# Moving the next expert's gather and transposes ahead of a tail, in an attention and mixture-of-experts kernel on one core

## The chip, the core and the metric

The kernel runs on one core of one Trainium2 chip. The metric is device time in microseconds (us) for one execution. A core has five engines that run side by side, each through its own instructions in program order, and that wait for each other by semaphores: PE (TensorE, the matrix unit; the profile shows its weight loads apart, as PEld), DVE (VectorE), ACT (ScalarE), POOL (GpSimd) and SP (SyncE, which here only issues DMAs). "SPq" in the profile is SP's queue.

## What is computed

The reference is a linear attention followed by a mixture of experts, each token going to two of eight experts:

```python
kv = np.einsum('bhsd,bhse->bhde', k, v)
out = np.einsum('bhsd,bhde->bhse', q, kv)
x = out / sqrt(mean(out * out) + 1e-6) * g_norm        # -> x: (4608, 512)
noisy = x @ w_gate + log1p(exp(x @ w_noise)) * noise   # 8 logits a token
top2, top2_w = the two largest and their softmax
for e in range(8):
    for k in range(2):
        mask = top2[:, k] == e
        h = np.maximum(x[mask] @ w1[e], 0.0)            # 512 -> 1024
        out[mask] += top2_w[mask, k, None] * (h @ w2[e])  # 1024 -> 512
```

Batch 8, 8 heads, 576 positions, head size 64: 4608 tokens of 512 values. The routing depends on the data, so how many tokens an expert gets is known only when the kernel runs (1152 on average).

## The kernel before, in words

**Two phases.** In the first 200 us or so the attention is computed, the logits, the routing, and the normalized tokens are written to memory (xs); the first units of expert 0 run inside it. After that the experts run one after the other. Only this second part matters here.

**Units and stages.** An expert's tokens are held in ten slots of 128 tokens (tiles). They are worked in units (list `units`, L344 to L349): experts 1 to 7 have two full units of four tiles and a tail of two, which I call A, B and T; expert 0 has four full units of two tiles and a tail. A unit goes through `gather` (L358: one indirect DMA a tile, issued from POOL, fetches token rows from xs into xg; five buffers), `halves` (L368: ACT casts a tile to half precision, POOL subtracts to get the remainder, both go to xh; four buffers), `xpose` (L375: one DMA transpose a tile, issued from SP, puts xh into xT; there are two xT buffers, which successive units alternate), `l1` (L414: first layer, matmuls at L427, evacuated from PSUM by ACT at L432 and DVE at L433 into hT) and `l2` (L465: second layer, matmuls at L473, ACT scales the result by the gate into y at L494, and `scatter`, L401, adds it to the output by an indirect DMA with addition from POOL, L405). PSUM tiles for all of this rotate over six buffers (`ps_tile`, L354).

A tail holds what is left of an expert's tokens. Its matmuls stand in a switch over the number of tokens in steps of 32 (L451), from none to 256, so a tail is short.

**Order of the work.** The program is issued in one order by the loop at L818; each engine takes its own part of it. For unit u it issues the gather of unit u+1, l1(u) and then l2(u-1). Around the tail the stages on PE follow each other as: l1(A), l2 of the tail before, l1(B), l2(A), l1(T), l2(B), l1 of the next expert's A. `l1` and `l2` are generators. A full unit yields 16 times in each of them (8 times for a unit of two tiles), a tail TY times in `l1` and twice in `l2`. After each yield the loop calls `fill()` (L772), which issues one step of background work.

**Halves and transposes** of unit u+1 are issued inside l1(u), after step XH = 5 and the next (L844). In a tail's l1 there are too few steps for that, so they follow after its last step (L846).

**Background work** is a queue of generators (`bg`). For the next expert it holds `locate` (L756), which finds the expert's tokens: it compares routing numbers on DVE (L309 to L314), counts with small matmuls into M (L322) and makes the lists of indices idx, row and gate (`finish`, L329). Then comes `prepare` (L750), which runs `weights` (L218). For each of the two raw weight matrices it takes the largest value (DVE, L225), spreads a scale over partitions by a small matmul of a diagonal dg (PE, L236, read by DVE at L238) and splits the float32 weights into two half-precision parts, a high one by ACT (L259) and a low one by DVE (L261, L263). A generator may yield a number n, and then the next n - 1 calls of `fill` do nothing for it.

**Raw weights** have one buffer for each layer (rw, 2 MB), filled by four DMAs of 512 KB from SP: `load_w1` (L207, DMAs at L210) and `load_w2` (L212, L216). The buffer is free when the last chunk has been split, so a load waits on SP for DVE's last split (L263), and whatever stands behind it in SP's queue waits too. In `weights`, the load of the next expert's first layer is issued right after the split of this one's first layer (L285), that of the second right after the split of the second (L293).

Of the kernel before, what the change touches and what calls it, by code (L numbers as in the profile page):

```python
# [24 lines left out]
E, FF = 8, 1024  # L25
# [21 lines left out]
XH = 5  # L47
FE = 2
GB, HB = 5, 4
GRAIN, TY, HINT = 32, 4, 5  # L50
PZ = 4


# [1 line left out]
def attention_moe(ctx: ExitStack, tc: tile.TileContext, kvm, kvr, qt, gn, wgn, noise, w1, w2, out):  # L55
# [7 lines left out]
    raw = ctx.enter_context(tc.tile_pool(name="raw", bufs=1))  # L63
# [141 lines left out]
    WT, RW, late = {}, {}, {}  # L205

    def load_w1(e):  # L207
        r = RW[e, 0] = raw.tile([P, 4, 1024], F32, name="rw")
        for c in range(4):
            SP.dma_start(r[:, c], w1[e, c * P:(c + 1) * P, :])  # L210

    def load_w2(e):  # L212
        r = RW[e, 1] = late.get("raw", raw).tile([P, 4, 1024], F32, name="rw")
        v = w2[e].rearrange("(c f p) d -> c p f d", f=2, p=P)
        for c in range(4):
            SP.dma_start(r[:, c].rearrange("p (f d) -> p f d", f=2), v[c])  # L216

    def weights(e, pool, lo, slack=0):  # L218
        WT[e] = w = {}
        sc = lists.tile([P, 8], F32, name="sc")  # L220

        def scale(o, src, mul):
            mx = lists.tile([P, 4], F32, name="mx")
            for c in range(4):
                V.tensor_reduce(mx[:, c:c + 1], src[:, c], axis=AX.X, op=OP.max, apply_absolute_value=True)  # L225
                yield
            V.tensor_reduce(sc[:, o:o + 1], mx, axis=AX.X, op=OP.max)
            if mul is not None:
                V.tensor_scalar(sc[:, o:o + 1], sc[:, o:o + 1], mul, None, op0=OP.mult)
            al = lists.tile([P, 1], F32, name="al")  # L230
            dg = lists.tile([P, P], F32, name="dg", bufs=1)
            V.tensor_scalar(dg, ident, sc[:, o:o + 1], None, op0=OP.mult)
            yield
            yield
            ps = ps_tile([P, P])
            T.matmul(ps, onef, dg, start=True, stop=True)  # L236
            yield
            V.tensor_reduce(al, ps, axis=AX.X, op=OP.max)  # L238
            V.tensor_scalar(al, al, 1e-30, 1e30, op0=OP.max, op1=OP.min)
            bi = lists.tile([P, 2], I32, name="bi")  # L240
            V.tensor_scalar(bi[:, 0:1], al.bitcast(I32), 0x7F800000, None, op0=OP.bitwise_and)
            V.tensor_scalar(sc[:, o + 1:o + 2].bitcast(I32), bi[:, 0:1], -1.0, float(257 << 23), op0=OP.mult, op1=OP.add)  # L242
            V.tensor_scalar(sc[:, o + 2:o + 3].bitcast(I32), bi[:, 0:1], 1.0, float(-(3 << 23)), op0=OP.mult, op1=OP.add)
            if mul is not None:
                V.scalar_tensor_tensor(sc[:, o + 1:o + 2], sc[:, o + 1:o + 2], -1.0, g, op0=OP.mult, op1=OP.mult)  # L245
            yield

        def split(src, hi, lw, s):
            if lo is G:
                for c in range(5):  # L250
                    if c:
                        G.tensor_tensor(lw[:, c - 1], src[:, c - 1], hi[:, c - 1], OP.subtract)
                    if c < 4:
                        A.activation(src[:, c], src[:, c], AF.Copy, scale=s)
                        A.activation(hi[:, c], src[:, c], AF.Copy)
                    yield
                return
            for c in range(4):
                A.activation(hi[:, c], src[:, c], AF.Copy, scale=s)  # L259
                if c:  # L260
                    lo.scalar_tensor_tensor(lw[:, c - 1], src[:, c - 1], s, hi[:, c - 1], op0=OP.mult, op1=OP.subtract)  # L261
                yield
            lo.scalar_tensor_tensor(lw[:, 3], src[:, 3], s, hi[:, 3], op0=OP.mult, op1=OP.subtract)  # L263
            yield
            yield

        if (e, 0) not in RW:
            load_w1(e)
            yield WY
            for _ in range(slack):  # L270
                yield
        r1 = RW.pop((e, 0))
        yield from scale(0, r1, gabs)
        w["w1h"] = pool.tile([P, 4, FF], F16, name="w1h")
        w["w1l"] = pool.tile([P, 4, FF], F16, name="w1l")
        yield from split(r1, w["w1h"], w["w1l"], sc[:, 1:2])
        for _ in range(min(slack, 3)):
            yield
        if (e, 1) not in RW:
            load_w2(e)  # L280
            yield WY
            for _ in range(slack):
                yield
        elif e + 1 < E:
            load_w1(e + 1)  # L285
        r2 = RW.pop((e, 1))
        yield from scale(3, r2, None)
        V.tensor_scalar(sc[:, 6:7], sc[:, 2:3], sc[:, 5:6], -1.0 / XS, op0=OP.mult, op1=OP.mult)
        w["c"] = sc[:, 6:7]
        w["w2h"] = pool.tile([P, 4, FF], F16, name="w2h")  # L290
        w["w2l"] = pool.tile([P, 4, FF], F16, name="w2l")
        yield from split(r2, w["w2h"], w["w2l"], sc[:, 4:5])
        if "raw" in late and e + 1 < E:  # L293
            load_w2(e + 1)
        for k in ("w2h", "w2l"):
            w[k] = w[k].rearrange("p c (f d) -> p (c f) d", f=2)

# [27 lines left out]
    def scale_gates(e, c):  # L325
        if "c" in WT.get(e, ()):
            V.tensor_scalar(LG[e][:, c], LG[e][:, c], WT[e]["c"], None, op0=OP.mult)
# [16 lines left out]
    units = []  # L344
# [9 lines left out]
    def ps_tile(shape):  # L354
        rot[0] = (rot[0] + 1) % 6
        return (psa if "ps" not in late or rot[0] < 2 else late["ps"]).tile(shape, F32, name="pp")
# [35 lines left out]
    def clear():  # L392
        r = next(blank, None)
        if r is not None:
            zeroed.append(A.dma_start(ov[:, r], zrow).ins)
            return True
# [124 lines left out]
    ready, loaded = {0}, set()  # L521
# [223 lines left out]
    late["ps"] = ctx.enter_context(tc.tile_pool(name="psb", bufs=4, space=PSUM))  # L745
    psl = ctx.enter_context(tc.tile_pool(name="psl", bufs=1, space=PSUM))
    bg = deque()
    hold = [0]

    def prepare(e):  # L750
        yield from weights(e, wts_b if e % 2 else wts_a, V)
        if e in ready:
            scale_gates(e, slice(0, CAP))
        loaded.add(e)

    def locate(e):  # L756
        M = psl.tile([P, 5 * CAP], F32, name="M")
# [10 lines left out]
    def background(e):  # L768
        yield from locate(e)
        yield from prepare(e)  # L770

    def fill():  # L772
        hold[0] -= 1
        if bg and hold[0] <= 0:
            try:
                hold[0] = next(bg[0]) or 1
            except StopIteration:
                bg.popleft()

    bg.append(prepare(1))  # L780
    k = 0
    while side:
# [35 lines left out]
    for u in range(EARLY, len(units) + 1):  # L818
        if u < len(units):
            e, tiles, tail = units[u]  # L820
            if u + 1 < len(units):
                en = units[u + 1][0]
                while en not in ready:
                    fill()
                if (u + 1, units[u + 1][1][0]) not in XG:
                    gather(u + 1)
                if units[u + 1][2]:
                    RV[en] = [nc.values_load(arms[0:1, i, en:en + 1], engines=(ET.PE,), min_val=0, max_val=m)
                              for i, m in enumerate((2 * P // GRAIN, 2))]
            if u > EARLY:  # L830
                while clear():
                    pass
                scatter()
            while e not in loaded:
                fill()
            if tiles[0] == 0 and e + 1 < E:
                bg.append(locate(e + 1))
                bg.append(prepare(e + 1))
            todo = deque([halves, xpose] if u + 1 < len(units) and u + 1 not in XT else ())
            for i, _ in enumerate(l1(u)):  # L840
                if i == HINT and u and units[u - 1][2]:
                    tc.switch_hint({ET.PE: RV[units[u - 1][0]][1]}, 3, label=f"down{units[u - 1][0]}")
                fill()
                if todo and i >= XH:  # L844
                    todo.popleft()(u + 1)
            while todo:  # L846
                todo.popleft()(u + 1)
        if u > EARLY:
            for i, _ in enumerate(l2(u - 1)):
                if i == HINT and u + 1 < len(units) and units[u + 1][2]:  # L850
                    en = units[u + 1][0]
                    tc.switch_hint({ET.PE: RV[en][0]}, 256 // GRAIN + 1, label=f"up{en}")
                if i == HINT and u + 1 == len(units):
                    tc.switch_hint({ET.PE: RV[e][1]}, 3, label=f"down{e}")
                fill()


# [69 lines left out]
```

## Time and profile before

| | us |
|---|---|
| median of 3 runs | 1046.17 |
| lowest, highest | 1027.74, 1051.88 |
| the profiled execution | 1023.48 |
| its span, first to last instruction | 1021.6 |
| mean granted PE clock, as a share | 0.957 |

The profile's page lists busy time by engine. "Busy" for PE is modelled, so a busy PE isn't PE at its peak. Other views show who waited for whom (engine, line, what it waited for: total us, times, longest), the instructions of an engine in order of time (start, duration, engine, line, operation, output <- inputs, shape, count, and in brackets the idle time before and what ended it), and busy times cut by stretches of the span (length, then busy us and instructions of each engine, the granted PE clock as a share, the mean busy share of the DMA engines, which can exceed 1, and GB/s).

### The profile page before, as it was taken

To read this page: it belongs to the slowest core of one execution; us is meant where nothing else is said; L and a number is where in the kernel's file an instruction comes from. 1 tells how busy PE (TensorE), PEld (TensorE's weight loads), DVE (VectorE), ACT (ScalarE), POOL (GpSimd) and SP (SyncE) were. 2 spreads that over 40 slices of the span, in tenths; PEclk is the share of its full clock that TensorE was granted. 3 is DMA by queue.
4 is the path that set the end of the run, shared out by engine and by line. 5 is a ranking of instruction groups with operands and counts; after the bars stand their busy time and mean duration, and the time that the engine had idled before them with its cause. 6 is when DMAs were issued, how large, how long until landed. Compare 5 with 4: busy or idle time off the path is not lost. (4 is left out here: it accounts for less than half of the span.)

```text
span 1021.6 us, 15198 instructions
## 1 busy us (share of the span) xinstructions
PE 920.9 (90%) x5962; PEld 516.6 (51%) x5962; DVE 497.8 (49%) x1046; ACT 331.1 (32%) x573; POOL 379.6 (37%) x398
## 2 busy tenths in 40 slices
PE   9957797898999979997999889997999989999995
PEld 8846774574444534463445434463444344644452
DVE  2869988855456333840555345632375257411100
ACT  2736662243223321341224322332133223421211
POOL 0214543445522642145223632263224541552222
PEclk9979988999999979998999989998999999999998
DMA  9988966966834864259244953357327842473224
GB/s 347 335 299 289 273 250 228 293 140 169 205 64 114 151 124 60 68 129 205 43 62 119 183 113 64 109 153 115 52 55 198 172 87 34 92 128 57 36 41 56
DMA packets 140826, 145.88 MB, mean 143 GB/s; under 512 B 90784, under 2 KB 99104, under 8 KB 140704
## 3 DMA queue, kind: packets, MB, share of 16 engines
q1 hardware_dynamic: 108192, 82.25, 30.3%
q0 software_dynamic: 17920, 41.95, 21.3%
q10 hardware_dynamic: 14592, 19.93, 5.8%
q8 instruction: 91, 1.49, 0.6%
q14 instruction: 31, 0.25, 0.1%
HBM read 83.02 MB, written 40.11 MB: 121 GB/s over the span
## 5 line engine op out<-in xcount | busy, mean ns | idle before, releaser
L427 PE MATMUL pp<-xT,w1h 128*128 128x512 f16 (+5 forms) x1600 | 370.2, 329 | 36.1 <-DMA xT<-xh 28.7
L473 PE MATMUL pp<-w2h,hT 128*128 128x512 f16 x1200 | 364.8, 381 | 1.9 <-ACT hT L432 1.2
L433 DVE SCALAR_TENSOR_TENSOR hT<-pp,hT 128x512 f16<-128x512 f32 x160 | 107.4, 687 | 404.1 <-ACT hT L432 404.1
L473 PEld LDWEIGHTS <-hT 128*128 128x128 f16 x1800 | 176.0, 98 | 212.8 <-issue 5.4
L405 POOL DMA_INDIRECT out_rows<-y,row x80 | 130.1, 1626 | 371.5 <-ACT y L494 354.6
L427 PE MATMUL pp<-xT,w1l 128*128 128x512 f16 (+5 forms) x800 | 257.5, 328 | 0.0
L473 PE MATMUL pp<-w2l,hT 128*128 128x512 f16 x600 | 228.7, 381 | 0.0
L427 PEld LDWEIGHTS <-w1h 128*128 128x128 f16 x1600 | 150.6, 99 | 147.2 <-issue 49.4
L432 ACT ACTIVATE hT<-pp 128x512 f16<-128x512 f32 x160 | 92.7, 597 | 317.5 <-PE pp L427 315.0
L372 POOL TENSOR_TENSOR xh<-xg,xh 128x512 f16<-128x512 f32 x80 | 114.4, 1456 | 118.7 <-ACT xh L371 118.7
L494 ACT ACTIVATE y<-pp,gate 128x512 f32<-128x512 f32 x80 | 53.9, 686 | 252.5 <-PE pp L473 226.8
L427 PEld LDWEIGHTS <-w1l 128*128 128x128 f16 x800 | 79.5, 99 | 58.0 <-issue 5.8
L364 POOL DMA_INDIRECT xg<-xs,idx x80 | 79.9, 998 | 35.1 <-issue 23.0
L225 DVE TENSOR_REDUCE mx<-rw 128x1 f32<-128x1024 f32 x64 | 74.4, 1208 | 11.3 <-DMA rw<-w 11.3
L585 PE MATMUL big<-kvbd,qt 128*128 128x160 f32 (+1 forms) x320 | 58.9, 337 | 14.9 <-ACT kvbd L577 12.5
L612 POOL TENSOR_TENSOR x<-o,ss 128x512 f32<-128x512 f32 x36 | 38.6, 1073 | 64.6 <-DVE ss L606 57.4
L585 PEld LDWEIGHTS big<-kvbd,qt 128*128 128x128 f32 (+1 forms) x320 | 49.3, 201 | 17.3 <-ACT kvbd L577 13.4
L371 ACT ACTIVATE xh<-xg 128x512 f16<-128x512 f32 x80 | 46.0, 629 | 23.0 <-DMA xg<-xs,idx 19.1
L309 DVE TENSOR_TENSOR oa<-jb,lnb 128x1152 bf16<-128x1152 bf16 x32 | 52.6, 1642 | 0.0
L259 ACT ACTIVATE w2h<-rw,sc 128x1024 f16<-128x1024 f32 x32 | 35.8, 1146 | 6.0 <-DVE sc L242 6.0
L404 POOL MEMSET tick<- 1x1 f32 x80 | 37.2, 465 | 0.0
L259 ACT ACTIVATE w1h<-rw,sc 128x1024 f16<-128x1024 f32 x32 | 34.5, 1138 | 1.7 <-DVE sc L245 1.7
(134 smaller groups left out, 570.8 us busy)
## 6 DMA issues: line engine op xcount, KB each, us to landing
rw<-w SPq DMA_DIRECT2D x64, 512.0 KB, 6.5
kvc<-kvm SPq DMA_DIRECT2D x32, 512.0 KB, 7.2
xs<-x ACTq DMA_DIRECT2D x36, 256.0 KB, 4.0
out_rows<-zrow ACTq DMA_DIRECT2D x36, 256.0 KB, 3.9
qt<-qt SPq DMA_DIRECT2D x8, 640.0 KB, 7.2
qt<-qt SPq DMA_DIRECT2D x8, 512.0 KB, 8.5
kvr<-kvr SPq DMA_DIRECT2D x4, 512.0 KB, 8.2
xg<-xs,idx POOLq DMA_INDIRECT x80, 4.4
```

Source lines behind the costliest of these rows:

```text
L225: V.tensor_reduce(mx[:, c:c + 1], src[:, c], axis=AX.X, op=OP.max, apply_absolute_value=True)
L259: A.activation(hi[:, c], src[:, c], AF.Copy, scale=s)
L309: V.tensor_tensor(oa, jb[:, None, :].to_broadcast([P, n, P]), lnb[:, s, e:e + 1].to_broadcast([P, n, P]), OP.is_equal)
L364: G.indirect_dma_start(out=x, out_offset=None, in_=src, in_offset=bass.IndirectOffsetOnAxis(ap=LI[e][:, t:t + 1], axis=0))
L372: G.tensor_tensor(x[:, 1], XG[u, t], x[:, 0], OP.subtract)
L405: d = G.indirect_dma_start(out=out, out_offset=bass.IndirectOffsetOnAxis(ap=LS[e][:, t:t + 1], axis=0), in_=y, in_offset=None, compute_op= ...
L427: T.matmul(ps[:, f % ps.shape[1], 0:n], w[wn][:, c, f * P:(f + 1) * P], x[:, xo + c, 0:n], start=(c == 0 and k == 0), stop=(c == HP - 1 an ...
L432: A.activation(h[:, 0, f:f + nf, 0:n], ps, AF.Relu)
L433: V.scalar_tensor_tensor(h[:, 1, f:f + nf, 0:n], ps, 0.0, h[:, 0, f:f + nf, 0:n], op0=OP.max, op1=OP.subtract)
L473: T.matmul(ps, h[:, hk, f, i * P:(i + 1) * P], w[wn][:, f], start=(f == 0 and k == 0), stop=(f == 7 and k == 2))
L494: A.activation(y, ps, AF.Copy, scale=LG[e][:, t:t + 1])
L585: T.matmul(TL[t, "ps"][r0:r0 + n, hp, 0:160], q[:, hp, s0 - o:s0 - o + n], kvbd[b % 2][:, hp, :], start=True, stop=True)
```

## The change

Three things change, in four places. TY goes from 4 to 1, so a tail's l1 issues one background step. A new number AFT = 4 is yielded ahead of the load of the next first-layer weights and of the next second-layer weights; the latter moves from the end of `weights` to the end of `prepare`. And while l2(u) of an A unit is issued (the loop's unit is B, the next one is a tail), the gather, the halves and the transposes of the unit behind the tail are issued at steps 0, 8 and 15.

```diff
-GRAIN, TY, HINT = 32, 4, 5
+GRAIN, TY, HINT, AFT = 32, 1, 5, 4
...
         elif e + 1 < E:
+            yield AFT
             load_w1(e + 1)
...
         yield from split(r2, w["w2h"], w["w2l"], sc[:, 4:5])
-        if "raw" in late and e + 1 < E:
-            load_w2(e + 1)
...
+    AHEAD = {0: gather, 8: halves, 15: xpose}
...
     def prepare(e):
         yield from weights(e, wts_b if e % 2 else wts_a, V)
         if e in ready:
             scale_gates(e, slice(0, CAP))
         loaded.add(e)
+        if e + 1 < E:
+            yield AFT
+            load_w2(e + 1)
...
             for i, _ in enumerate(l2(u - 1)):
...
+                if u + 2 < len(units) and units[u + 1][2] and i in AHEAD:
+                    while units[u + 2][0] not in ready:
+                        fill()
+                    AHEAD[i](u + 2)
                 fill()
```

The loop's own gather and its halves and transposes skip a unit that has them already (L825, L839). An expert 0 unit has two tiles and its l2 eight steps, so of the three only the one at step 0 happens there.

## The prediction

> **What bounds the kernel now.** I read the page first, then PE's waits from 200 us on (where the experts run one after the other), then the stretches around those waits, then the queue behind them.
>
> ```profile
> PE 920.9 (90%) x5962; PEld 516.6 (51%) x5962; DVE 497.8 (49%) x1046; ACT 331.1 (32%) x573; POOL 379.6 (37%) x398
> ```
>
> PE is the only engine near its limit; the others have half their time free. So what counts is what PE waits for, and how fast it runs. Its waits from 200 to 1012 us (who waits for whom, total us, times, longest):
>
> ```profile
> PE pp L427 <- DMA xT<-xh: 28.7, 5, 8.2
> PE pp L236 <- DVE dg L232: 8.6, 6, 1.5
> PE pp L427 <- issue: 5.1, 3, 2.5
> PE pp L236 <- DVE hT L433: 3.6, 1, 3.6
> ```
>
> One wait dominates: first-layer matmuls (L427) wait five times for the transposed activations xT. I call an expert's units A and B (four tiles each) and T (the tail); a stage is "l1" or "l2" of a unit. PE's order is l1(A), l2 of the T before, l1(B), l2(A), l1(T), l2(B), then the next l1(A). All five waits are at that last hand-over, l2(B) to l1(A). The next view cuts the span there: five pairs of a gap and the l1(A) behind it (experts 2 to 6), then l2 of expert 0's last full unit, l1(A) of expert 1, then l2(A), l1(T), l2(B) of expert 4, and l2(B) of expert 6.
>
> ```profile
> core 0: us, PE busy (x) PEld busy (x) DVE busy (x) ACT busy (x) POOL busy (x), PEclk, DMA share, GB/s
> 359.04:365.81 6.77, 0.00 (x1) 0.03 (x1) 0.00 (x0) 0.69 (x1) 4.51 (x4) 0.66 1.26 199
> 365.81:389.73 23.92, 23.92 (x114) 10.54 (x115) 12.30 (x15) 6.25 (x11) 6.99 (x6) 0.88 0.45 94
> 473.40:479.77 6.37, 0.00 (x1) 0.03 (x1) 0.00 (x0) 0.69 (x1) 4.40 (x4) 0.80 1.28 149
> 479.77:503.04 23.27, 23.27 (x115) 10.31 (x115) 12.31 (x15) 6.25 (x11) 7.09 (x7) 0.91 0.37 93
> 584.20:592.38 8.18, 0.00 (x0) 0.03 (x1) 0.00 (x0) 0.69 (x1) 5.46 (x5) 0.64 1.14 137
> 592.38:615.66 23.28, 23.28 (x115) 10.34 (x115) 12.31 (x15) 6.25 (x11) 6.03 (x5) 0.91 0.34 85
> 695.16:700.48 5.32, 0.00 (x1) 0.03 (x1) 0.00 (x0) 0.69 (x1) 3.57 (x3) 0.87 1.29 149
> 700.48:724.32 23.84, 23.84 (x115) 10.45 (x116) 12.31 (x15) 6.25 (x11) 7.93 (x7) 0.89 0.40 92
> 801.27:803.78 2.51, 0.00 (x1) 0.03 (x1) 0.00 (x0) 0.69 (x1) 1.46 (x1) 1.00 1.16 190
> 803.78:826.64 22.86, 22.86 (x114) 10.27 (x115) 12.31 (x15) 6.25 (x11) 10.04 (x10) 0.93 0.53 113
> 244.93:257.14 12.21, 12.21 (x50) 5.04 (x47) 9.29 (x12) 6.92 (x9) 8.20 (x6) 0.86 0.34 66
> 259.25:280.42 21.17, 21.17 (x115) 9.82 (x115) 9.58 (x15) 6.48 (x11) 10.16 (x10) 1.00 0.82 222
> 644.02:664.96 20.94, 20.94 (x99) 9.71 (x98) 14.05 (x19) 8.99 (x10) 5.14 (x6) 1.00 0.52 139
> 664.96:674.28 9.32, 9.32 (x101) 9.31 (x100) 0.00 (x0) 1.81 (x3) 5.46 (x5) 1.00 0.56 125
> 674.28:695.16 20.88, 20.88 (x98) 9.30 (x96) 8.08 (x8) 7.15 (x12) 12.05 (x11) 1.00 0.74 170
> 883.49:904.21 20.72, 20.72 (x99) 9.41 (x97) 6.82 (x7) 7.14 (x12) 10.87 (x11) 1.00 0.60 97
> ```
>
> Two losses are to be seen: the gaps, in which PE does nothing while the DMA share is above 1, and the stages behind them, which the granted clock (PEclk below 1) makes longer than the same stage at full clock (21.17 us for expert 1). The last row is the control: expert 6's l2(B) ends at 904.21 and the next l1(A) follows with no gap, though the tail ahead of it is as long as expert 4's. What differs is SP's queue:
>
> ```profile
> 680.63 1.92 SPq L216 DMA_DIRECT2D rw<-w  x4
> 682.66 12.34 SPq L384 DMA_TRANSPOSE xT<-xh  x4
> ```
> ```profile
> 888.75 6.19 SPq L384 DMA_TRANSPOSE xT<-xh  x4
> ```
> ```profile
> SPq L216 <- DVE w2l L263: 123.9, 5, 27.7
> ```
>
> For experts 1 to 5 the load of raw second-layer weights (L216, four DMAs of 512 KB) stands in SP's queue ahead of the transposes; it waits there for the split that frees its buffer (123.9 us in five waits), and the transposes then take 12.34 us to issue. Expert 6 has no more weights to load: 6.19 us, and no gap.
>
> **The change, part by part.** *Gather, halves and transposes of the next A move from the tail to l2(A)* (gather at step 0, halves at 8, transposes at 15). Per expert these are 4 gather DMAs on POOL, 4 casts on ACT, 4 subtractions on POOL and 4 transposes on SP, no more and no fewer than before. The rows for them (engine timelines, then DMA issues with KB each and median us to landing):
>
> ```profile
> 631.71 2.32 POOL L372 TENSOR_TENSOR xh<-xg,xh 128x512 f16<-128x512 f32 x2 [3.55 <-ACT xh L371]
> ```
> ```profile
> 677.89 7.13 POOL L372 TENSOR_TENSOR xh<-xg,xh 128x512 f16<-128x512 f32 x4 [5.04 <-ACT xh L371]
> ```
> ```profile
> 677.16 2.21 ACT L371 ACTIVATE xh<-xg 128x512 f16<-128x512 f32 x4
> ```
> ```profile
> rw<-w SPq DMA_DIRECT2D x64, 512.0 KB, 6.5
> ...
> xg<-xs,idx POOLq DMA_INDIRECT x80, 4.4
> out_rows<-y,row POOLq DMA_INDIRECT x80, 5.6
> xT<-xh SPq DMA_TRANSPOSE x76, 3.3
> ```
> ```profile
> 631.30 0.17 DVE L335 TENSOR_TENSOR idx<-la 128x10 int32<-128x10 f32 x1
> ```
> ```profile
> 671.91 0.95 POOL L364 DMA_INDIRECT xg<-xs,idx  x1 [0.30 <-issue]
> ```
>
> With expert 4's times: the index list is written at 631.30, and POOL is through the tail's subtractions at 634.03, so it can gather at once: four at 0.95 + 0.30 us (last row, now at 671.91) end at 639.0, landed by 643.4, before l2(A) starts at 644.02. Step 8 stands behind the second tile's copy y, 644.02 + 20.94/2 + 0.7 = 655.2; casts to 657.4; subtractions 4.6 to 7.1 us (1.16 to 1.78 each in the rows), so to 664.5 at most; four transposes at 1.5 us (6.19/4) issued by about 666, landed by 670. l1(A) of the next expert starts at 695.16 at the earliest: 25 us to spare, so the gap goes. On POOL the subtractions hold the third scatter of l2(A) back by up to 4 us, in a stage in which POOL is busy for 5.14 of 20.94 us; PE does not wait for scatters. On ACT the casts' 2.2 us lie between two copies 5.2 us apart. I cost both at nothing; without that cover it would be the 7.1 us.
>
> *The loads move four steps behind the splits.* I count the calls of the background generator for one expert: 16+2+16+16+4+16 = 70 before, 67 after (tail: one step). Locating takes 24; preparing 28 before, 36 after (two pauses of 4); two calls end the generators. 62 of 67: it still fits. Locating ends at step 6 of l1(B), 10 calls ahead of the gather. The broadcast matmul for w2 goes from step 11 of l2(A) to step 15, just ahead of the tail; the w2 split goes from the end of l2(A) and the tail to steps 0 to 4 of l2(B); its load from the tail's last step to step 10 of l2(B). SP is not paced by steps: it starts each load when the split is through.
>
> ```profile
> 649.49 1.28 DVE L263 SCALAR_TENSOR_TENSOR w1l<-rw,sc,w1h 128x1024 f16<-128x1024 f32 x1
> ```
> ```profile
> 678.42 2.18 DVE L263 SCALAR_TENSOR_TENSOR w2l<-rw,sc,w2h 128x1024 f16<-128x1024 f32 x1
> ```
>
> So w1's load stays at 650.8, in front of the moved transposes, and is landed about 8 us later (four at 0.5 us to issue, 6.5 to land), at 659, when the first of them starts; if they had to wait behind it, there are still 25 us. w2's load comes later than 680.6: after the tail's evacuation (677.3) DVE still has the scale and four chunks of 1.3 us, each behind an ACT chunk, so about 686, landed by 695, with the transposes long done. The next transposes on SP (unit B's) need casts inside l1(A), some 8 us after 695. Nothing is late next there. The broadcast matmul at its new place is not in the trace. Bounds: 0, as the w2 broadcasts of experts 2 to 7 now have no row among the waits (the six at 8.6 us are w1's in l1(B), with DVE busy evacuating), and 3.6 us, the one that stands behind a tail (expert 1's). It stays ahead of the tail and its scale is made four steps earlier: I take 0; the upper bound is 6 x 3.6 = 21.4 us.
>
> *Expert 0* has units of two tiles, whose l2 has 8 steps: only the gather moves, halves and transposes stay behind l1(T). But the pause moves expert 1's w2 broadcast (now the 3.56 us wait at 244.6 us) into the l2 behind it, and two ACT chunks away from ahead of the casts. That can save 3.6, the slow clock behind it ((1 - 0.86) x 12.21 = 1.7) and the gap at 257.14 (2.1): 0 to 7.4, I take 5, since the transposes become the later of the two.
>
> *The sum.* Gaps of experts 2 to 6: 6.77 + 6.37 + 8.18 + 5.32 + 2.51 = 29.15. Slow clock behind them, (1 - PEclk) x length: 2.87 + 2.09 + 2.10 + 2.62 + 1.60 = 11.28; as a check, the five lengths are 117.17, less 5 x 21.17 = 11.3. With 5 for expert 1: 45.4 us. The profiled execution took 1023.48 us (span 1021.6), so it would become 978. It was faster than the three runs (1027.74 to 1051.88, median 1046.17); the gaps depend on DMA, so I carry the difference over unscaled: 1046.2 - 45.4 = 1000.8, say **1001 us**.
>
> [...]
>
> **Rivals.**
>
> *The tail takes half of it back* (the 3.6 us at six broadcasts): for it, the one such wait near a tail; against it, all others in l2. 1046.2 - 45.4 + 21.4 = 1022.
>
> *The gap moves to l1(B).* If w2's load is released so late that it stands in front of unit B's transposes, the 29.15 + 11.28 come back there and only expert 1's 5 stay: 1041. It decides from a release later than about 8 us into l1(A), 703 in these times; I get 686.
>
> [...]
>
> **How the numbers follow.** Forecast 0.82, tail rival 0.06, l1(B) rival 0.05, ACT rival 0.04, anything else 0.03. The forecast's own range: terms 40.4 to 47.8, from the lowest and highest of the runs: 1027.7 - 47.8 = 980 to 1051.9 - 40.4 = 1012. Down to 972 for a median near the profiled execution (1023.5 - 47.8 = 976) and a little below; up to 1028 for the tail rival from the highest run (1051.9 - 24). A measurement here tells about 2% (21 us) from no change, so "faster" is below 1025: the forecast, most of the tail rival: 0.86. Within 2%: the l1(B) rival, the rest of the tail's, some of the others: 0.10. Slower: 0.04.
>
> **What would show it.** Right: no wait of L427 for xT at experts 2 to 6; PEclk 1.00 and about 21.2 us in their l1(A); on SP the four transposes of A ahead of the L216 load, some 25 us before use; gathers in l1(B). Wrong: a wait of L236 or of the tail's first matmul, a wait of L427 at l1(B), ACT's y waiting for xg, or hand-overs that still end on xT.

## The result, and the profile after

The changed kernel takes 981.63 us (median of 4 runs, 979.22 to 987.21); the kernel before took 1040.05 us (4 runs, 1027.74 to 1051.88). The ratio is 0.953, 95% interval 0.9446 to 0.9614: faster. It leaves out the executions counted as slow (here 1046.17 and 1051.88 us of the kernel before), so ratios here and below aren't the quotients of the medians beside them (0.944 here), and between groups the times are to be compared. The profiled execution took 979.22 us (span 977.3) against 1023.48 before, 44.3 us less.

Line numbers in the profile after are one lower from L294 on: L426 is the first layer (L427 before), L472 the second, L383 the transposes.

PE's waits from 200 to 1012 us of the changed kernel (total us, times, longest), to be held against the four rows of before:

```profile
PE pp L236 <- DVE dg L232: 6.2, 5, 1.5
PE pp L472 <- ACT xh L370: 4.1, 1, 4.1
PE pp L472 <- issue: 2.8, 1, 2.8
PE pp L426 <- issue: 2.6, 2, 1.4
PE pp L426 <- DMA xT<-xh: 2.5, 1, 2.5
PE pp L472 <- ACT hT L431: 1.5, 1, 1.5
```

The wait for xT was 28.7 us in five; one of 2.5 us is left, at 200 us, before the first hand-over. (The waits of 4.1, 2.8 and 1.5 us in L472 stand behind tails; more on them below.) The five l1(A) stages that stood behind the gaps, cut by stretches as before:

```profile
355.34:376.35 21.01, 21.01 (x114) 9.71 (x113) 12.31 (x15) 7.05 (x12) 11.62 (x10) 1.00 0.73 155
459.79:480.81 21.02, 21.02 (x115) 9.76 (x113) 12.31 (x15) 7.05 (x12) 11.90 (x10) 1.00 0.54 115
561.82:582.83 21.01, 21.01 (x114) 9.76 (x113) 12.31 (x15) 7.14 (x12) 11.89 (x10) 1.00 0.55 117
661.55:682.57 21.02, 21.02 (x115) 9.76 (x113) 12.31 (x15) 7.05 (x12) 11.90 (x10) 1.00 0.56 117
763.35:784.36 21.01, 21.01 (x114) 9.73 (x113) 12.30 (x15) 7.05 (x12) 11.90 (x10) 1.00 0.55 116
```

All at PEclk 1.00 and 21.0 us; before they took 22.9 to 23.9. SP's queue around expert 4's tail (l2(A) from 610.4, l1(T) from 631.4, l2(B) 640.7 to 661.6), and POOL's gathers for the next A (the last four of six in l1(B), which began at 588.5):

```profile
617.18 1.77 SPq L210 DMA_DIRECT2D rw<-w  x4
624.74 7.78 SPq L383 DMA_TRANSPOSE xT<-xh  x4
650.68 2.52 SPq L216 DMA_DIRECT2D rw<-w  x4
```
```profile
601.68 0.96 POOL L363 DMA_INDIRECT xg<-xs,idx  x1
602.95 0.95 POOL L363 DMA_INDIRECT xg<-xs,idx  x1 [0.30 <-issue]
604.20 0.95 POOL L363 DMA_INDIRECT xg<-xs,idx  x1 [0.31 <-issue]
605.45 0.95 POOL L363 DMA_INDIRECT xg<-xs,idx  x1 [0.30 <-issue]
```

The transposes stand ahead of the w2 load (L216), behind that of w1 (L210), and are issued by 632.5, 29 us before l1(A) needs them.

### The profile page after: what moved, and what is told of

Its sections match the earlier page's. It is cut to its first block, busy times and chain, and to the rows that moved or that the text cites. A ratio compares the mean times of both kernels' runs of the same rounds, so it can differ in the third digit from the quotient of the medians.

```text
span 977.3 us, 15167 instructions
## 1 busy us (share of the span) xinstructions
PE 909.1 (93%) x5962; PEld 513.8 (53%) x5962; DVE 483.9 (50%) x1046; ACT 331.0 (34%) x573; POOL 367.9 (38%) x398
## 3 DMA queue, kind: packets, MB, share of 16 engines
q0 software_dynamic: 17920, 41.95, 22.9%
## 4 chain that ended last, share of the span: by engine, by line
PE 56%; DVE 5%; issue 2%; ACT 1%; POOL 1%; POOLq 0%; ACTq 0%
PE pp L472 31%; PE pp L426 24%; DVE mx L225 2%; DVE hT L432 1%; POOL out_rows L404 1%; ACT hT L431 1%; PE M L321 0%; DVE gate L339 0%; PE pp L236 0%; DVE row L337 0%; POOLq L930 0%; DVE la L335 0%; DVE idx L334 0%; DVE la L333 0%; DVE la L332 0%
## 5 line engine op out<-in xcount | busy, mean ns | idle before, releaser
L472 PE MATMUL pp<-w2h,hT 128*128 128x512 f16 x1200 | 365.8, 382 | 9.9 <-ACT xh L370 4.1
L426 PE MATMUL pp<-xT,w1h 128*128 128x512 f16 (+5 forms) x1600 | 360.9, 322 | 5.1 <-issue 2.6
L472 PEld LDWEIGHTS <-hT 128*128 128x128 f16 x1800 | 176.3, 98 | 222.2 <-issue 10.7
L426 PE MATMUL pp<-xT,w1l 128*128 128x512 f16 (+5 forms) x800 | 252.8, 322 | 0.0
L472 PE MATMUL pp<-w2l,hT 128*128 128x512 f16 x600 | 229.2, 382 | 0.0
L426 PEld LDWEIGHTS <-w1h 128*128 128x128 f16 x1600 | 148.9, 98 | 109.8 <-issue 6.9
L371 POOL TENSOR_TENSOR xh<-xg,xh 128x512 f16<-128x512 f32 x80 | 102.2, 1431 | 50.8 <-ACT xh L370 48.3
L426 PEld LDWEIGHTS <-w1l 128*128 128x128 f16 x800 | 78.4, 98 | 54.5
L363 POOL DMA_INDIRECT xg<-xs,idx x80 | 82.8, 1035 | 38.2 <-issue 21.0
L611 POOL TENSOR_TENSOR x<-o,ss 128x512 f32<-128x512 f32 x36 | 38.6, 1072 | 65.6 <-DVE ss L605 58.4
L403 POOL MEMSET tick<- 1x1 f32 x80 | 40.4, 505 | 0.0
```

Of the source, the lines that this page charges most:

```text
L363: G.indirect_dma_start(out=x, out_offset=None, in_=src, in_offset=bass.IndirectOffsetOnAxis(ap=LI[e][:, t:t + 1], axis=0))
L371: G.tensor_tensor(x[:, 1], XG[u, t], x[:, 0], OP.subtract)
L426: T.matmul(ps[:, f % ps.shape[1], 0:n], w[wn][:, c, f * P:(f + 1) * P], x[:, xo + c, 0:n], start=(c == 0 and k == 0), stop=(c == HP - 1 an ...
L472: T.matmul(ps, h[:, hk, f, i * P:(i + 1) * P], w[wn][:, f], start=(f == 0 and k == 0), stop=(f == 7 and k == 2))
```

## The experiments

The theory was: the four transposes stood behind the w2 load in SP's queue, that alone made the gap, and the gap made the slow clock. All ratios are to the kernel before, timed on the same chip (medians of 1038.8, 1040.9 and 1045.0 us in the three groups: first four experiments, next four, last three), with 95% intervals. In the second group one execution of the kernel before took 1577.5 us, and the verdict of all four experiments of that group is on record as unclear, though three of the intervals lie wholly below 0.98.

### Each part alone

*The early gather, halves and transposes alone* (TY = 4, no pause, the load in its old place in the code):

```diff
+    AHEAD = {0: gather, 8: halves, 15: xpose}
...
+                    AHEAD[i](u + 2)
```

> Only the early gather, halves and transposes; the tail still issues four background steps and the loads stand where they stood. Theory: what costs is the order on SP, transposes behind the w2 load; here they are ahead of it, so the five gaps (29.2 us) and the slow clock behind them (11.3 us) go, and the profiled execution takes 978 to 988 us, within 1% of the whole change. Rival (the pauses and the shorter tail do part of it, because a load right behind the split blocks SP or the DMA engines): at least 10 us of gaps stay, 995 us or more.

Measured: 981.7 us, ratio 0.941 (0.933 to 0.949). The gaps of experts 2 to 6 are gone; expert 1's is as before (2.1 us). On SP the transposes come at 628.9, the w2 load at 650.3. As the theory had it.

*The pauses alone:*

```diff
+            yield AFT
             load_w1(e + 1)
...
-        if "raw" in late and e + 1 < E:
-            load_w2(e + 1)
...
+        if e + 1 < E:
+            yield AFT
+            load_w2(e + 1)
```

> Only the two pauses of four steps; gather, halves and transposes stay behind the tail. The w2 load moves from the tail's last step to step 7 of l2(B), so it is issued on SP behind the transposes. Theory (order on SP): expert 6 of the kernel before, with nothing in front of its transposes, had them landed 6 us ahead of use, so the gaps go here as well: 978 to 990 us. Rival (gather, casts and subtractions behind the tail are too late, and the early gather is what is needed): gaps of 3 us or more stay at four or five hand-overs, over 1000 us.

Measured: 991.4 us, ratio 0.951 (0.943 to 0.960), just outside the expected 978 to 990. No wait for xT is left at any hand-over, so the theory's main point held: moving the loads is enough. What is missing is in another place, the first row of PE's waits:

```profile
PE pp L236 <- DVE dg L232: 18.7, 7, 6.9
```

Two broadcast matmuls of w2, of experts 1 and 2 (4.6 and 6.9 us, at 246.8 and 343.0), now stand in PE's queue where their diagonal isn't ready. That is what the pauses cost while the tail still issues four steps, probably because they push background work back by four steps at a time. The whole change has the pauses too and has no wait at these broadcasts.

*The one-step tail alone*, one number:

```diff
-GRAIN, TY, HINT = 32, 4, 5
+GRAIN, TY, HINT = 32, 1, 5
```

> Only TY = 1: three background steps leave the tail, so the w2 load falls to step 2 of l2(B), behind the transposes in SP's queue, though only just. Theory (order on SP): the gaps go, 978 to 990 us. Rival (early gather needed): as before, 1015 us or more; rival (the pause is needed, as the load's 2 MB still meet the transposes on the DMA engines): gaps of 2 to 4 us stay, about 1000 us.

Measured: 979.7 us, ratio 0.941 (0.934 to 0.949). This edit does the whole of it. SP's queue at expert 4's hand-over, and PE's waits:

```profile
613.57 1.78 SPq L210 DMA_DIRECT2D rw<-w  x4
642.32 7.00 SPq L384 DMA_TRANSPOSE xT<-xh  x4
649.41 2.84 SPq L216 DMA_DIRECT2D rw<-w  x4
```
```profile
PE pp L236 <- DVE dg L232: 8.3, 6, 1.5
PE pp L427 <- issue: 3.4, 3, 1.3
PE pp L236 <- issue: 2.7, 1, 2.7
PE M L322 <- issue: 1.3, 1, 1.3
PE pp L427 <- DMA xT<-xh: 0.9, 1, 0.9
```

Here the gather is as late as before the change and the load follows 0.1 us behind the last transpose. Counted from ACT's first copy y of l2(B) (679.71 us before, 642.49 here), ACT's casts (677.16; 639.93) and POOL's subtractions (677.89; 640.67) stand at the same times to 0.01 us. What differs is what SP issues first, the load or the transposes. So neither the early gather nor the pause is needed; both rivals fell.

### The order undone

*The whole change, but the transposes behind the load again*: gather and halves stay early, the transposes go to step 15 of l2(B).

```diff
-    AHEAD = {0: gather, 8: halves, 15: xpose}
+    AHEAD = {0: gather, 8: halves}
...
-            todo = deque([halves, xpose] if u + 1 < len(units) and u + 1 not in XT else ())
+            todo = deque([halves, xpose] if u + 1 < len(units) and u + 1 not in XT and not (tail and e) else ())
...
+                if i == 15 and tail and e and u + 1 < len(units):
+                    xpose(u + 1)
```

> The whole change, except that the four transposes are issued at step 15 of l2(B), behind the w2 load in SP's queue; gather and halves stay early. Theory (order on SP): the load is released about 10 us into l2(B) (448.95 with l2(B) from 438.91 in the changed kernel's profile) and the transposes behind it take 12 us to issue, so they land 5 to 8 us after the end of l2(B): the gaps and the slow clock come back, about 1020 us (1010 to 1030). Rival (early gather and halves are what counts, SP's order is harmless): 978 to 988 us.

Measured: 1037.4 us, ratio 0.9992 (0.9958 to 1.0026): all of the gain is lost, more than expected. SP around expert 4's hand-over, and the first row of PE's waits:

```profile
661.69 1.77 SPq L210 DMA_DIRECT2D rw<-w  x4
695.18 2.29 SPq L216 DMA_DIRECT2D rw<-w  x4
697.58 12.62 SPq L383 DMA_TRANSPOSE xT<-xh  x4
```
```profile
PE pp L426 <- DMA xT<-xh: 50.3, 5, 16.4
```

The subtractions that make their data end at 672.5, 25 us ahead of the transposes, which still come too late. Together with the one-step tail alone this shows the cause from both sides. Four transposes take 12.62 us to issue behind the load, against 7.00 ahead of it. What makes them slower there no run shows.

### The clock behind the gap

*The kernel before, with 90 matmuls of zeros between l2(B) and l1(A) of experts 1 to 4* (extra work that nothing waits for; `keep_warm` is a helper that the kernel has already):

```diff
+            if u < len(units) and tail and 1 <= e <= 4:
+                keep_warm(90)
```

> The kernel before, with 90 extra 128-column matmuls of zeros into an unused PSUM region on PE between l2(B) and the next l1(A), for experts 1 to 4 (5.0 us of work inside gaps of 5.3 to 8.2 us; nothing waits for them). Theory (the slow clock follows PE's idleness, as a cost of its own beside the gap): the hand-over lasts as long as before, but l1(A) of experts 2 to 5 runs at PEclk 0.98 to 1.00 and takes 21.2 instead of 23.3 to 23.9 us: 9 to 10 us less than before, ratio 0.985 to 0.995. Rival (l1(A) is slow for another reason, such as the transposes or the raw load on the DMA engines at that time): PEclk stays near 0.9, ratio 1.00 to 1.01.

Measured: 1027.2 us, ratio 0.9936 (0.9867 to 1.0006): within the expected 0.985 to 0.995, but no change isn't excluded, so the time alone shows nothing. The profile tells more: the l1(A) of experts 2 to 5, and two of PE's wait rows.

```profile
366.29:389.03 22.74, 22.74 (x115) 10.20 (x116) 12.31 (x15) 6.25 (x11) 6.04 (x5) 0.93 0.38 98
479.80:500.97 21.17, 21.17 (x114) 9.85 (x115) 12.31 (x15) 6.25 (x11) 6.38 (x6) 1.00 0.41 105
594.99:617.72 22.73, 22.73 (x115) 10.18 (x115) 12.31 (x15) 6.25 (x11) 6.03 (x5) 0.93 0.30 67
703.07:724.24 21.17, 21.17 (x117) 9.84 (x115) 12.31 (x15) 6.25 (x11) 8.27 (x8) 1.00 0.51 103
```
```profile
PE pp L427 <- DMA xT<-xh: 16.7, 3, 7.9
...
PE pp L427 <- issue: 6.7, 4, 2.9
```

In this execution three of the four gaps were longer than the 5 us of filling (an estimate: 90 times the 0.056 us from one 128-column matmul to the next in the tail at 237 us of the changed kernel): 2.9 us of idleness remained ahead of the first stage, 2.3 ahead of the second, 7.9 ahead of the third, none ahead of the fourth. The stages behind 2.3 us and none ran at full clock (21.17 us), the two others lost 1.6 us each. So in these four stages the slow clock goes with PE's idleness, while SP issues the load and the transposes behind it at all four. (The first row's 16.7 us include 6.4 us at expert 1, which was not filled.)

### The rival that was slower

*Gather, halves and transposes all at step 15 of l2(A)*, so that ACT meets the casts while the gathers are still on their way:

```diff
-    AHEAD = {0: gather, 8: halves, 15: xpose}
+    def whole(u):
+        gather(u)
+        halves(u)
+        xpose(u)
+    AHEAD = {15: whole}
```

> The whole change, but gather, halves and transposes all at step 15 of l2(A), so that POOL gathers behind that stage's last scatter, and ACT meets the casts ahead of the tail's evacuation. Theory (ACT rival of the prediction: ACT stands at a cast until its gather has landed, and PE stops when the PSUM ring is out): the gather lands 8 to 12 us after the end of l2(A), the tail's evacuation waits for that, and the second tile of l2(B) waits 2 to 4 us for a PSUM buffer (8 us for expert 5, whose tail is empty); no wait for xT: 995 to 1010 us. Rival (six PSUM buffers hide it): 978 to 988 us.

Measured: 994.7 us, ratio 0.967 (0.961 to 0.974), just under what was expected (995 to 1010) and 13 us over the changed kernel's 981.6. ACT's row, and PE's:

```profile
ACT xh L370 <- DMA xg<-xs,idx: 58.3, 27, 7.0
...
PE pp L236 <- DVE dg L232: 12.5, 6, 5.3
```

ACT does stand at the casts. But PE felt it less than my estimate of 8 us of waiting and 2.3 of slow clock for each hand-over (worked out from the times before: the casts and the third copy through at 680.2, that copy's PSUM buffer needed by the tail at 672). In l2(B) it waited 4.7 us in expert 5, whose tail is empty, and 1.3 us in expert 3; in the other four it has no such wait, so there the six PSUM buffers seem to have covered it. The largest single wait is the broadcast of expert 2's w2 (5.3 us, in l2(B) of expert 1), perhaps late because ACT and DVE were; that wasn't tested. So the mechanism exists, at 6.0 us of waits over six hand-overs, 1 us each and not 10. Even with all of the 13 us put down to it, it would be near 2.

### Without the pause; and the first load out of the way

*The change without the two pauses* (AHEAD and TY = 1 stay):

```diff
-            yield AFT
             load_w1(e + 1)
...
-            yield AFT
             load_w2(e + 1)
```

> The early gather and the tail with one step, without the two pauses: the loads stand right behind the splits. Theory (order on SP alone counts, the pauses do nothing): within 0.7% of the whole change, 972 to 984 us; a little faster if anything, since expert 1's background work is not pushed back. Rival (the pauses keep SP or the DMA engines free for the transposes): 990 us or more, with a wait for xT.

Measured: 979.0 us, ratio 0.951 (0.947 to 0.956), as the theory had it: the pauses bring nothing.

*The first paused load moved to the start of expert 1*, to test the wait of 4.1 us in the changed kernel's rows above. There PE's sequencer, which the profile lists under PEld, stands in the branch that leaves the tail's switch:

```diff
-            load_w1(e + 1)
+            if e > 1:
+                load_w1(e + 1)
...
             if tiles[0] == 0 and e + 1 < E:
+                if e == 1:
+                    load_w1(2)
```

> The whole change, and in addition the very first of the paused loads (first layer of expert 2, 2 MB, issued at 228 us and in flight while expert 0's tail runs) is issued at the start of expert 1's unit A instead. Theory (PE's branch out of the tail's switch, 5.2 us for expert 0's tail against 0.3 for most others, waits for instructions that are fetched through busy DMA engines): that branch takes under 1 us, the 4.1 us wait at 242.8 us and the 1.7 us of slow clock behind it go, 4 to 6 us less than the whole change. Rival (the branch is slow because the tail is short or for another reason that has nothing to do with the load): the branch stays at 4 to 5 us, time within 2 us of the whole change.

The branch's rows (operation, count and ns): the changed kernel, then this experiment, expert 0's tail and then expert 1's.

```profile
L930 PEldq COMPARE_BRANCH  x1: 5177/5177/5177, 237.5 to 237.5; - x1
```
```profile
L933 PEldq COMPARE_BRANCH  x1: 2502/2502/2502, 240.6 to 240.6; - x1
```
```profile
L933 PEldq COMPARE_BRANCH  x1: 5947/5947/5947, 329.7 to 329.7; - x1
```

Measured: 980.6 us, ratio 0.952 (0.946 to 0.958): no gain. The branch fell to 2.5 us, not under 1, and expert 1's (2.9 us in the changed kernel) rose to 5.9. The one-step tail alone, whose first load is where it was, had 3.7 at that place, and over all 13 profiles that branch took 1.9 to 5.9 us, so 2.5 says little. That this load makes the branch long isn't borne out.

The half of the theory on fetching can be held against the traces. The profile's DMA view has a queue that it calls "instruction". In the changed kernel one packet of it (0.02 MB) stands inside each of the branches at 237.5 (5.2 us), 277.8 (3.6 us) and 331.3 (2.9 us), near 240.3, 278.6 and 331.6, and the branch ends 2.4 to 2.9 us later; the branches of 0.3 us at 437.4 and 639.0 have none from 2 us ahead to their end. (Some long ones have it up to 1.3 us ahead, as this experiment's of 2.5 us.) The one at 277.8 was long with the DMA engines nearly idle (share 0.02), so that one wasn't long because they were busy. These are times that lie close together; whether the branch waits for the packet no run shows.

### Once more, on one chip

*The kernel before, unchanged:*

> The kernel before, unchanged, for a second profile of it. Its executions spread from 1021 to 1053 us, those of the changed kernel from 979 to 987. Theory: the spread is in the gaps behind the w2 load and the slow clock after them; a profile of an execution at 1035 us or more shows gaps of experts 2 to 6 of 35 us or more in place of 29.2, and the rest of the span stays at about 980 us less the changed kernel's own differences. Rival: the spread lies in the first 200 us or the stages themselves; the gaps stay at 29 us whatever the time.

Measured: 1046.0 us, ratio 0.999 (0.993 to 1.005), with a profile of an execution of 1047.43 us (span 1045.7). Its gaps of experts 2 to 6, with the first l1(A) behind them:

```profile
356.13:377.57 21.44, 0.00 (x0) 0.03 (x1) 0.00 (x0) 0.69 (x1) 5.45 (x5) 0.56 1.15 129
377.57:401.21 23.64, 23.64 (x114) 10.39 (x115) 12.31 (x15) 6.25 (x11) 6.03 (x5) 0.89 0.30 46
484.97:491.31 6.34, 0.00 (x0) 0.03 (x1) 0.00 (x0) 0.69 (x1) 4.38 (x4) 0.77 1.24 199
595.42:613.18 17.76, 0.00 (x0) 0.03 (x1) 0.00 (x0) 0.69 (x1) 5.45 (x5) 0.56 1.03 149
717.25:723.33 6.08, 0.00 (x0) 0.03 (x1) 0.00 (x0) 0.69 (x1) 4.12 (x4) 0.77 1.24 170
823.94:826.08 2.14, 0.00 (x0) 0.03 (x1) 0.00 (x0) 0.69 (x1) 1.09 (x1) 1.00 1.21 205
```

21.44 + 6.34 + 17.76 + 6.08 + 2.14 = 53.8 us, 24.6 more than in the first profile, and the span is 24.1 us longer. So in these two executions the difference in time lies in the gaps, and the DMA share is above 1 through all of them. In the longest, SP had issued the four transposes by 364.7 us, 13 us before l1(A) could start. From 362 to 376 us the DMA engines were shared between POOL's queue (q0, gathers and scatters) and SP's (q1):

```profile
q0 software_dynamic: 531, 1.43, 72.8%
q1 hardware_dynamic: 1760, 0.44, 41.3%
```

So the load isn't all that late transposes meet: POOL's transfers are under way there too. How much of the delay is due to which was not tested.

*The one-step tail alone and the whole change* (no edit beyond those above):

> TY = 1 alone once more, timed against the whole change on one chip. Theory: the whole gain is the place of the w2 load behind the transposes, which this one edit gives; equal to the whole change within 0.7%, a little faster (2 to 4 us), since expert 1's background work is not pushed back by pauses. Rival: slower than the whole change by more than 0.7%.

> The whole change once more, on the same chip as TY = 1 alone. Theory: 979 to 985 us; TY alone is equal or 2 to 4 us faster. Rival: the whole change is faster by 5 us or more, because the early gather gives the hand-over slack that some executions need.

Measured: 980.5 us, ratio 0.939 (0.934 to 0.945), and 985.2 us, ratio 0.944 (0.938 to 0.950). They are equal within 0.7%; the one number by itself is at least as good as the whole change, 4.7 us ahead on this chip, with intervals that overlap. One difference in the two profiles is the branch behind expert 1's tail: 6.0 us in the whole change, where PE waits 4.7 us, and 0.3 us in the one-step tail alone.

## Why the prediction was right, point by point

**The gaps** (29.15 us expected to go): right, by the mechanism named. No l1(A) of experts 2 to 6 waits, and undoing the order alone brings the waits back. One reading was loose: the five waits in the row for xT are those of experts 1 to 5 (6.77 + 6.37 + 8.18 + 5.32, and 2.10 at expert 1), not the five pairs shown; the 2.51 us of expert 6 stand under "issue" in the profile. They went as well, and with the order undone the wait there is one for xT (6.2 us).

**The slow clock** (11.28 us): right. The five stages took 117.17 us and take 105.07, so 12.1 us. The one gap that was wholly filled was followed by a stage at full clock.

**The new places** (at no cost): right. For expert 4 the gathers ended 17.9 us into l1(B) (17.7 worked out), the last transpose was issued 22 us into l2(A) (22), the w2 load came 10.0 us into l2(B) (11.7). POOL's third scatter of l2(A) came 1.1 us later (17.8 us into the stage against 16.8) and PE didn't see it. The w2 broadcast ahead of the tail doesn't appear among the waits, so the bound of 0 was the right one.

**Expert 1** (5 us, 0 to 7.4): the size was near, the reason partly wrong. From l1 of expert 0's third unit to l1(A) of expert 1 it took 259.25 - 201.48 = 57.8 us and takes 255.04 - 200.59 = 54.5, 3.3 less. The gap of 2.1 us went, and 1.5 us ahead of the tail, which I hadn't counted. But the wait of 3.56 us that I put down to a broadcast behind the tail goes by the times with the branch out of the switch: in the kernel before it takes 4.5 us from 239.9, and PE goes on 0.2 us after its end. With the broadcast moved away, the first matmul of l2 waits 4.1 us at the same place, until 0.1 us after the end of the branch (5.2 us, the row above), and the profile names ACT. The releaser in that row is inferred; the times fit the end of the branch.

**What I didn't see**: two such branches took longer in this execution, behind the tails of experts 1 and 5 (waits of 1.5 and 2.8 us against 0 and 0.6, and 1.7 us of slow clock behind the second). They take back 5.4 us. The rest of the 44.3 us in the two profiles, 44.3 - 29.2 - 12.1 - 3.3 + 5.4 = 5.1 us, lies in pieces of at most 1.6 us, the first 200 us (0.9) and the end (1.5) among them.

**From the profile to the median**: here the step was weak. For the profiled execution I had 978 us, and it was 979.2. That it came so near is luck in part: 1.7 us too much for expert 1 and 5.4 us not seen stand against 0.8 us more from the clock and 5.1 us in small pieces. For the median I carried the 45.4 us over unscaled, to 1001, and it was 981.6: between the medians 58.4 us went. The gaps were 29.2 us in one execution and 53.8 in another, with the DMA engines shared as shown above. The kernel before varies by 2% for that reason at least in part, and the profile happened to show one of its fastest executions. Without the gaps the runs lie within about 1%, and the change saves what each execution loses. The range (972 to 1028) took it in from the side of the profiled execution.

**The reach of the parts**: I costed three edits together and named the order on SP, but didn't say that each of them alone reverses it. By the count of steps it could be read: with TY = 1 the w2 load falls from the tail's last step to step 2 of the next stage, behind the transposes.

## What to carry to other kernels

In a queue that issues both bulk loads and small transfers somebody waits for, look at which comes first at each hand-over: here one number that put four transposes ahead of a 2 MB load was worth 6%, and everything else in the change nothing that could be measured. The gaps of the kernel before were 29.2 us in one execution and 53.8 in another, with the DMA share above 1 in both; what such a gap is worth is to be judged from several executions. A kernel whose times scatter more than its fellow's (1027.74 to 1051.88 us against 979.22 to 987.21) may have one. Times that don't scatter are no sign of the opposite: with the order undone PE waited 50 us for xT, and the ten runs lay within 0.8%. When an idle row names an engine that has long been done, look for a branch on the waiting engine's own sequencer: here 5.2 us of one stood over a wait of 4.1 us that the row gave to ACT.

## What the runs showed of the hardware

PE's clock: 2.51 us of idleness (expert 6, before), 2.9 us (a gap filled in part) and 2.14 us (expert 6, the kernel before once more) were each followed by a stage at PEclk 0.92 or 0.93, 2.3 us (another gap filled in part) and 2.10 us (expert 1, before) by one at 1.00. The changed kernel's wait of 2.51 us for xT, up to 200.59, was followed by 20 us at 1.00, so the same length came out both ways and didn't decide by itself.

The branch that leaves a switch took PE's sequencer 0.3 us in most tails. In all 13 profiles it was long at two places, behind expert 0's tail (1.9 to 5.9 us) and behind the first layer of expert 5's empty tail (4.5 to 6.6 us). Behind expert 1's tail it was 2.9 and 6.0 us in the two profiles of the changed kernel and 5.9 with the first load moved, and 0.3 to 0.4 us in the other ten; why isn't shown.
